# Rows of maxima one visit sooner, and a new order of the first instructions, in a decay-attention and expert kernel on one core

## The chip, the cores and the metric

The kernel runs on one core of one Trainium2 chip. The metric is the time of one execution on the device, in microseconds; the times shown are medians of several executions. Five engines work beside each other, each through its own row of instructions in a fixed order: TensorE (PE, matmuls; PEld are its weight loads), VectorE (DVE), ScalarE (ACT), GpSimd (POOL) and SyncE (SP), which here issues all DMAs. An instruction waits for what it needs of other engines, and all that stands behind it in its engine's row waits with it.

## The reference

Inputs are q, k, v of shape (8, 8, 576, 64) and f of shape (8, 8, 576), float32, and two weights, w_in (512 x 2048) and w_out (2048 x 512), which come as float64. Cut to what matters:

```
scores = matmul(q, k^T) / sqrt(64)
cum    = cumsum(log(clip(f, 1e-4, 1)))
scores = where(causal, -1e9, scores + cum[:, None] - cum[None, :])
scores = scores - max(scores)
attn   = exp(scores) / (sum(exp(scores)) + 1e-9)
y      = matmul(attn, v)                    # 8 x 8 heads
x      = y laid out as 4608 tokens x 512
h      = x @ w_in
g      = h * clip(h + 3, 0, 6) / 6
out    = g @ w_out
```

## The kernel before, in words

The kernel works through 68 **visits** (the list `VH`). Visits 0 to 3, "A", take two heads of batch 0 each and only their first 256 rows; visits 4 to 11, "B", take the other 320 rows of heads 0 to 7; visits 12 to 67, "F", take one whole head each of batches 1 to 7. Batch 0 is cut in two so that its first 256 tokens are ready early for the expert part, the MoE.

One visit consists of these steps:

- `load_x` (L409, L414): q and k of the visit come by DMA into ST. `load_c` (L420 to L430): the rows of the decay sums come into TK; for visits 0 and 1 they come straight from the tile `cs`, which DVE makes at L174 and L175, four DMAs in all.
- `parts` (L449, L450): POOL copies k into TK and q into TQ, rounded to the matmul's format. `rests` (L456 to L461): the rounded values are sent by DMA into T7 and T1, and POOL subtracts them from the unrounded ones, which leaves the low parts.
- For visits 0 to 11, `natural`: PE multiplies TQ by TK (L487, tile pn, one position of a row to a partition), and DVE takes the masked maximum of each 128 rows (L493, in pieces "junk") into MC. `max_rows`: PE transposes MC (L502, tile ptm), DVE negates it (L504, tile mr), and SP sends it as one row into partition 96 of TQ (L505).
- `scores`: PE multiplies again, the other way round, now with the row of maxima among the operands (L551), adds the products of the low parts (L552) and the mask (L554), into ps; ACT takes the exponential. For F visits `rows` does the work in another way: PE makes pn (L611, L614), DVE the masked maxima (L622, L628), ACT the exponential (L634, L648), DVE or POOL the split in high and low halves (L651, L657, L662).
- `av`: PE multiplies by v (L694 to L705, tile pav); DVE scales and splits the result (L726 to L738). `x_move` (L751, L755): DMA transposes bring it to the layout in which the expert part reads it.

The weights come in 32 chunks through a few tiles named ring, w and gT: a DMA (L238), an ACT step on the float64's upper half (L251), a shift (L252) and an or (L253) on DVE that make it float32, its squares for the scale (L257). Once the scale of all w_in is known (the reductions at L279, the transposition L184, the matrix eye at L317), PE makes w_in's low halves (L287, L288), DVE those of w_out (L295). v is loaded by L355 to L357, its largest value found at L366, and it is split at L400.

The expert part goes in units: h (PE L777 to L779, then ACT and DVE L783 to L788) and the output (PE L824 to L826, tile po). `done` appends the units of a half batch to a list, and `fill` takes some of them at many places of a visit, by a credit that each place adds to. `moe_out` of batch 0 first runs through what is left of the weights' work (`wq`).

What stands where in an engine's row is not the order of this text alone: the framework's scheduler takes the instructions in the order in which they are written as priorities and simulates when each can run, and each engine's row is what comes out. `tc.issue_after(x)` keeps what is issued in it behind x. One new order in the text can thus move instructions far behind it.

The loop over the visits, in the old kernel: at visit i it issues `load_x(i+3)`, `load_c(i+2)`, the first scores of visit i, `rests(i+1)`, `parts(i+2)`, then `max_rows(i+1)` in the middle, `natural(i+2)` in two halves, and last `av` of visit i-1. The `x_move` and `done` of a visit come in the middle of the visit after its `av` (`pend_x`).

Of the kernel before, what the change touches and what calls it, by code (L numbers as in the profile page):

```python
# [11 lines left out]
F32 = mybir.dt.float32  # L12
# [3 lines left out]
ALU = mybir.AluOpType  # L16
# [4 lines left out]
def kernel(  # L21
# [137 lines left out]
    def decay():  # L159
# [15 lines left out]
        nc.vector.scalar_tensor_tensor(  # L175
            cs[:, 1, :], cum, -8.0, cs[:, 0, :].bitcast(F32), op0=ALU.mult, op1=ALU.subtract
        )
        yield
# [63 lines left out]
    def w_decode(i, k, slots):  # L242

        slot = slots[k % len(slots)]
        f32 = w_chunk(i, k)[1]
        if wide:
            i32 = f32.bitcast(I32)
            hf = slot.bitcast(F32).rearrange("p (n t) -> p n t", t=2)[:, :, 1]
            lo = slot.rearrange("p (n t) -> p n t", t=2)[:, :, 0]

            nc.scalar.activation(f32, hf, AF.Prelu, scale=2.0 ** -112, alpha=2.0 ** 32)  # L251
            nc.vector.tensor_scalar(i32, i32, 3, None, op0=ALU.logical_shift_left)  # L252
            nc.vector.scalar_tensor_tensor(  # L253
                i32, lo, 29, i32, op0=ALU.logical_shift_right, op1=ALU.bitwise_or
            )
        if i == 1 or not GRAM[k // NCC]:
            nc.scalar.activation(  # L257
                slot.bitcast(F32)[:, :CW], f32, AF.Square,
                accum_out=wsum[:, NW * i + k:NW * i + k + 1],
            )  # L260
# [183 lines left out]
    def parts(v):  # L444
# [5 lines left out]
        nc.gpsimd.tensor_scalar(TQ[i][0:D, 0:nq], s[0:D, q0:q0 + nq], **one)  # L450
# [47 lines left out]
    def max_rows(v):  # L498
# [3 lines left out]
        nc.tensor.matmul(pt[:m, :P], MC[v % 2][:, 0:m], identr, start=True, stop=True)  # L502
# [3 lines left out]
        small.append(d.ins)  # L506

# [385 lines left out]
    next(dec)  # L893
    load_c(0)
    parts(0)
# [4 lines left out]
    init_qk(1, nc.gpsimd if INIT_POOL[1] else nc.vector)  # L900
    load_c(1)
    parts(1)
    for i in range(NL):
        nc.gpsimd.memset(T1[i].bitcast(F32)[:, S:], 0.0)
    max_rows(0)
    rests(0)
# [3 lines left out]
    natural(1, 0)  # L910
    if W_ORDER == 2:
        next(w_in_q)
    init_qk(2, nc.gpsimd if INIT_POOL[2] else nc.vector)
    nc.gpsimd.memset(v_chunk(0, 4)[64:], 0.0)
# [44 lines left out]
    for i, (kind, n) in enumerate(VH):  # L959
# [27 lines left out]
        if i + 1 < NV and VH[i + 1][0] != "F":  # L987
            max_rows(i + 1)
# [24 lines left out]
        fill(1)  # L1013
        if prev is not None:
            av(*prev)
            if VH[prev[0]][0] == "A" or VH[prev[0]][1] % 2 == 1:
                pend_x = prev[0]
        if n == H:
            v_split(n // 2)
# [45 lines left out]
```

## Time and profile before

| what | value |
| --- | --- |
| median of 3 executions | 1073.61 us (1069.77 to 1073.86) |
| the profiled execution's own time | 1069.33 us |
| its span, first to last instruction | 1067.5 us |
| granted TensorE clock, mean | 0.988 |
| PE busy | 1006.3 us (94%), 7650 matmuls |
| DVE busy | 731.1 us (68%) |
| ACT busy | 587.3 us (55%) |
| POOL busy | 403.4 us (38%) |
| DMA | 133.78 MB, mean 125 GB/s |

The windows view gives, for stretches of the span, the busy time of each engine with the count of instructions, the granted TensorE clock (1.00 is full), the mean busy share of the 16 DMA engines, and what they moved. The waits view gives an engine's idle time by what ended it: in all, how often, the longest. A timeline row is: start, duration, engine, line, operation, tiles; in brackets the idle time before it and what ended that. A row of the groups view has the busy time and the mean in ns of one after the first bar, the idle time before it after the second. Tiles' numbers are left out in all of them.

### The profile page before, as it was taken

How to read it: one execution, taken by the hardware profiler on the slowest of the kernel's cores; microseconds unless marked ns; L12 is line 12 of the kernel's file. 1: busy time of each engine (PE TensorE's matmuls, PEld its weight loads, DVE VectorE, ACT ScalarE, POOL GpSimd, SP SyncE). 2: the span in 40 equal slices, each digit the busy share in tenths (PEclk: the TensorE clock that was granted, in tenths of full speed). 3: DMA queues.
4: the chain of work that ended last, by engine and by line, in shares of the span. 5: the costliest groups of instructions: out<-in, count | busy, mean ns of one | idle time of the engine just before them, and what ended most of it. 6: DMA issues, size and time to landing. Idle time of an engine off the chain costs nothing.

```text
span 1067.5 us, 21157 instructions
## 1 busy us (share of the span) xinstructions
PE 1006.3 (94%) x7650; PEld 598.0 (56%) x7650; DVE 731.1 (68%) x1887; ACT 587.3 (55%) x1189; POOL 403.4 (38%) x505
## 2 busy tenths in 40 slices
PE   2799977899999999999999999999999999999897
PEld 1577844665555755555555755555555755444543
DVE  6978899996876768866886668846895677105300
ACT  4778666764764557545654557635764566115301
POOL 8343466443443444344443444534443330000000
PEclk9989989999999999999999999999999999999999
DMA  8965647955856776667575766566557554010000
GB/s 240 308 187 194 151 109 145 220 114 118 169 116 134 139 153 124 113 148 165 118 134 118 158 140 119 118 136 167 119 112 145 103 100 74 12 40 1 1 20 30
DMA packets 259155, 133.78 MB, mean 125 GB/s; under 512 B 226948, under 2 KB 228540, under 8 KB 259052
## 3 DMA queue, kind: packets, MB, share of 16 engines
q1 hardware_dynamic: 259052, 132.44, 55.7%
q8 instruction: 60, 0.98, 0.4%
q14 instruction: 43, 0.35, 0.1%
HBM read 47.93 MB, written 9.73 MB: 54 GB/s over the span
## 4 chain that ended last, share of the span: by engine, by line
PE 76%; DVE 12%; ACT 5%; issue 4%; DMA 2%; POOL 1%; SPq 0%; DVEq 0%; ACTq 0%; POOLq 0%
PE po L824 9%; PE po L826 9%; PE po L825 9%; PE ph L777 9%; PE ph L778 9%; PE ph L779 9%; PE pn L611 3%; PE pn L614 3%; DVE pp L622 2%; DVE ring L651 2%; PE po_r L826 1%; PE pav L698 1%; ACT pp L634 1%; PE po_r L824 1%; PE po_r L825 1%
## 5 line engine op out<-in xcount | busy, mean ns | idle before, releaser
L634 ACT ACTIVATE pp<-pp,nb 128x192 f32<-128x192 f32 x280 | 138.6, 552 | 170.3 <-DVE nb L628 150.8
L777 PE MATMUL ph<-xT,w 128*128 128x512 f16 (+1 forms) x576 | 198.8, 357 | 2.5 <-DVE r L786 2.4
L825 PE MATMUL po<-w,gT 128*128 128x512 f16 x512 | 192.6, 382 | 8.0 <-DVE w L295 8.0
L779 PE MATMUL ph<-xT,w 128*128 128x512 f16 (+1 forms) x576 | 198.0, 356 | 0.0
L778 PE MATMUL ph<-xT,w 128*128 128x512 f16 (+1 forms) x576 | 197.8, 356 | 0.0
L651 DVE TENSOR_TENSOR ring<-pp,ring 128x128 f16<-128x128 f32 (+2 forms) x216 | 138.0, 650 | 85.6 <-ACT ring L648 84.7
L824 PE MATMUL po<-w,gT 128*128 128x512 f16 x512 | 190.4, 383 | 5.8 <-DVE r_r L813 2.7
L826 PE MATMUL po<-w,gT 128*128 128x512 f16 x512 | 192.4, 383 | 0.0
L622 DVE CUSTOM_DVE_ANT_0 pp<-pn,W 128x192 f32<-128x192 f32 x280 | 123.3, 482 | 29.3 <-PE pn L614 28.0
L461 POOL TENSOR_TENSOR T<-ST,T 64x576 fp32r<-64x576 f32 (+1 forms) x68 | 100.9, 1483 | 107.2 <-DMA T<-TK 85.8
L786 DVE SCALAR_TENSOR_TENSOR r<-r,ph 128x512 f32<-128x512 f32 (+1 forms) x144 | 89.1, 620 | 61.4 <-ACT r L783 60.6
L611 PE MATMUL pn<-TK,TQ 68*128 68x192 f32 x336 | 124.8, 385 | 3.8 <-issue 2.2
L788 DVE TENSOR_TENSOR gT<-r,gT 128x512 f16<-128x512 f32 (+1 forms) x144 | 111.6, 781 | 22.0 <-ACT gT L787 20.6
L614 PE MATMUL pn<-T,T 128*128 128x192 f32 x336 | 115.2, 368 | 0.2 <-POOL T L461 0.2
L783 ACT ACTIVATE r<-ph,bias_r,SC 128x512 f32<-128x512 f32 (+1 forms) x144 | 103.9, 725 | 19.2 <-PE ph L779 17.1
L648 ACT CAST ring<-pp 128x192 f16<-128x192 f32 x280 | 114.2, 449 | 0.0
L787 ACT CAST gT<-r 128x512 f16<-128x512 f32 (+1 forms) x144 | 81.4, 567 | 59.6 <-DVE r L786 59.3
L449 POOL TENSOR_SCALAR TK<-ST 64x576 fp32r<-64x576 f32 (+1 forms) x68 | 49.2, 724 | 167.8 <-PE pn L611 142.9
L657 POOL TENSOR_TENSOR ring<-pp,ring 128x128 f16<-128x128 f32 x96 | 61.0, 636 | 116.1 <-ACT ring L648 75.2
L458 POOL TENSOR_TENSOR T<-ST,TQ 64x576 fp32r<-64x576 f32 (+2 forms) x68 | 95.2, 1400 | 17.7 <-PE pn L614 11.1
L826 PEld LDWEIGHTS <-gT 128*128 128x128 f16 x560 | 54.8, 98 | 74.5 <-issue 15.1
L825 PEld LDWEIGHTS <-gT 128*128 128x128 f16 x560 | 54.9, 98 | 66.5 <-issue 11.9
(158 smaller groups left out, 2010.2 us busy)
## 6 DMA issues: line engine op xcount, KB each, us to landing
ST<-in_qk_dram SPq DMA_DIRECT2D x64, 288.0 KB
T<-TK SPq DMA_DIRECT2D x64, 144.0 KB
ring<-in_w_out_dram SPq DMA_DIRECT2D x16, 512.0 KB
out_dram<-o SPq DMA_DIRECT2D x32, 256.0 KB
T<-TQ SPq DMA_DIRECT2D x56, 144.0 KB
vst<-in_vS_dram SPq DMA_DIRECT2D x7, 1040.0 KB
ring<-in_w_in_dram SPq DMA_DIRECT2D x9, 512.0 KB
w<-in_w_in_dram SPq DMA_DIRECT2D x7, 512.0 KB
```

Source lines behind the costliest of these rows:

```text
L611: nc.tensor.matmul(dst, TQ[i][0:D + 4, qs], TK[i][0:D + 4, a:e], start=True, stop=False)
L614: nc.tensor.matmul(dst, T7[j][:, qs], T1[j][:, a:e], start=False, stop=True)
L622: nc.vector.tensor_tensor_reduce(pp[:r, w:w + kw], pn[:r, o:o + kw], W[:r, 4 * P + r - kw:4 * P + r], 1.0, -3.0e38, ALU.add, ALU.max, accu ...
L634: nc.scalar.activation(x_, x_, AF.Exp, bias=nb[:r, e0 + x:e0 + x + 1], scale=0.125)
L648: nc.scalar.copy(hl[:r, h0[c]:h0[c] + kw], pp[:r, at[c]:at[c] + kw])
L651: eng.tensor_tensor(hl[:r, a:a + c * P], pp[:r, at[c] + 64:at[c] + kw], hl[:r, h0[c] + 64:h0[c] + kw], op=ALU.subtract,)
L777: nc.tensor.matmul(ph, w1[0][:, cc, fs_], xh, start=(cc == 0), stop=False)
L778: nc.tensor.matmul(ph, w1[0][:, cc, fs_], xl, start=False, stop=False)
L779: nc.tensor.matmul(ph, w1[1][:, cc, fs_], xh, start=False, stop=(cc == NCC - 1))
L824: nc.tensor.matmul(po, g[:, 0, fc, ts_], w2[:, fc, 0, :], start=(fc == 0), stop=False)
L825: nc.tensor.matmul(po, g[:, 0, fc, ts_], w2[:, fc, 1, :], start=False, stop=False)
L826: nc.tensor.matmul(po, g[:, 1, fc, ts_], w2[:, fc, 0, :], start=False, stop=(fc == NFC - 1))
```

## The change

Four things are changed. First, the shifts of the first three w_in chunks are kept behind the second row of `cs`. Second, the start has another order: POOL makes `parts(0)` before it clears the tiles of visits 1 and 2 or makes `rests(0)`, `max_rows(0)` is issued right after `natural(0, 0)`, `natural(1, 0)` is kept behind its transposition, and `max_rows(1)` is issued before the loop. Third, the loop issues `max_rows(i+2)` at the end of visit i, where it issued `max_rows(i+1)` in the middle: the rows of maxima of batch 0 are made and sent one visit sooner. Fourth, the last A pair's `x_move` and `done` come right after its `av`, not one visit later. The work itself is the same.

```diff
-        nc.vector.scalar_tensor_tensor(
+        last = nc.vector.scalar_tensor_tensor(
             cs[:, 1, :], cum, -8.0, cs[:, 0, :].bitcast(F32), op0=ALU.mult, op1=ALU.subtract
         )
+        small.append(last.ins)
...
-            nc.vector.tensor_scalar(i32, i32, 3, None, op0=ALU.logical_shift_left)
+            with tc.issue_after(after_cs) if i == 0 and k < 3 else nullcontext():
+                nc.vector.tensor_scalar(i32, i32, 3, None, op0=ALU.logical_shift_left)
...
     next(dec)
+    after_cs = small.pop()
     load_c(0)
-    parts(0)
+    p0 = parts(0)
...
     natural(0, 0)
-    init_qk(1, nc.gpsimd if INIT_POOL[1] else nc.vector)
+    m0 = max_rows(0)
+    with tc.issue_after(p0):
+        rests(0)
+        init_qk(1, nc.gpsimd)
+        for i in range(NL):
+            nc.gpsimd.memset(T1[i].bitcast(F32)[:, S:], 0.0)
     load_c(1)
-    parts(1)
-    for i in range(NL):
-        nc.gpsimd.memset(T1[i].bitcast(F32)[:, S:], 0.0)
-    max_rows(0)
-    rests(0)
+    p1 = parts(1)
     load_x(2)
     load_v(0)
     nc.sync.dma_start(scr, cs.bitcast(F32))
-    natural(1, 0)
-    if W_ORDER == 2:
-        next(w_in_q)
-    init_qk(2, nc.gpsimd if INIT_POOL[2] else nc.vector)
-    nc.gpsimd.memset(v_chunk(0, 4)[64:], 0.0)
+    with tc.issue_after(m0):
+        natural(1, 0)
+    max_rows(1)
+    with tc.issue_after(p1):
+        init_qk(2, nc.gpsimd)
+        nc.gpsimd.memset(v_chunk(0, 4)[64:], 0.0)
...
         ph = next(sg)
-        if i + 1 < NV and VH[i + 1][0] != "F":
-            max_rows(i + 1)
...
+        last_a = prev is not None and VH[prev[0]] == ("A", NPAIR - 1)
         if prev is not None:
             av(*prev)
             if VH[prev[0]][0] == "A" or VH[prev[0]][1] % 2 == 1:
                 pend_x = prev[0]
+        if last_a:
+            x_move(pend_x)
+            done(pend_x)
+            pend_x = None
+        if front:
+            max_rows(i + 2)
```

How the rows move on the engines, at three places. A number behind a tile's name tells copies of a tile apart; after the change the code's lines stand two or three lower.

SP at the start, before, from the cs rows of visit 0 to v's loads: the row of maxima of visit 0 (TQ0 from mr_0) stands ahead of the three loads from in_vS_dram.

```order
L430 DMA TK0_96<-cs_121 2x1x256 x2
L430 DMA TK1_97<-cs_121 2x1x256 x2
L456 DMA T70_101<-TQ0_93 64x512
L457 DMA T10_99<-TK0_96 64x512
L909 DMA decay_dram<-cs_121 64x1152
L238 DMA ring2_125<-in_w_in_dram 128x1024
L238 DMA w2_115<-in_w_in_dram 128x1024
L457 DMA T11_100<-TK1_97 64x512
L424 DMA TK2_98<-decay_dram 2x2x256
L456 DMA T71_102<-TQ1_94 64x512
L505 DMA TQ0_93<-mr_0_186 1x4x128
L355 DMA v16_111<-in_vS_dram 128x3x520
```

The same place on SP after:

```order
L432 DMA TK0_96<-cs_121 2x1x256 x2
L432 DMA TK1_97<-cs_121 2x1x256 x2
L357 DMA v16_111<-in_vS_dram 128x3x520
L358 DMA xT1_118<-in_vS_dram 128x520
L359 DMA xT1_118<-in_vS_dram 64x520
L914 DMA decay_dram<-cs_121 64x1152
L458 DMA T71_102<-TQ1_94 64x512
L459 DMA T11_100<-TK1_97 64x512
L239 DMA ring2_125<-in_w_in_dram 128x1024
L239 DMA w2_115<-in_w_in_dram 128x1024
L426 DMA TK2_98<-decay_dram 2x2x256
L411 DMA ST0_103<-in_qk_dram 128x2x256
```

The loads of v and the reload of ST0 stand ahead of the row of maxima now, which is the next row behind these.

DVE before, about the first row of maxima (the ISA rows are the masked maxima of L493, which leave their result in MC0 for visit 0 and MC1 for visit 1):

```order
L493 ISA MC1_107 128x1
L504 TENSOR_SCALAR mr_0_186<-ptm_0_184 4x128
L493 ISA junk_1_1_205,MC1_107<-pn_1_0_198,W_88 128x256
L493 ISA MC1_107 128x1
L252 TENSOR_SCALAR gT_116<-gT_116 128x512
L493 ISA junk_1_2_207,MC1_107<-pn_1_0_198,W_88 128x128
L493 ISA MC1_107 128x1
L253 SCALAR_TENSOR_TENSOR gT_116<-ring2_125,gT_116 128x512
L493 ISA junk_1_3_209,MC1_107<-pn_1_0_198,W_88 128x256
```

DVE after, from the third to the last maximum of visit 0 and to its row:

```order
L495 ISA junk_0_2_169,MC0_106<-pn_0_0_160,W_88 128x128
L495 ISA MC0_106 128x1
L368 TENSOR_REDUCE vm0_246<-v16_111 128x1
L281 TENSOR_REDUCE wm0_283<-wsum_122 128x1
L495 ISA junk_0_3_171,MC0_106<-pn_0_0_160,W_88 128x256
L495 ISA MC0_106 128x1
L368 TENSOR_REDUCE vm0_246<-xT1_118 128x1
L188 TENSOR_SCALAR e_w00_287<-pt_w00_285 128x1
L506 TENSOR_SCALAR mr_0_175<-ptm_0_173 4x128
```

Both reductions of v (L368) stand ahead of the row mr_0 now; before, they came behind the maxima of visit 1.

PE before, where the first output matmuls (po_0_0) of the first MoE half begin: behind the natural scores of visit 13.

```order
L611 MATMUL pn_13_1_1759<-TK1_97,TQ1_94 128x448
L614 MATMUL pn_13_1_1759<-T11_100,T71_102 128x448
L824 LDWEIGHTS gT_116
L824 MATMUL po_0_0_1376<-w2_115,gT_116 128x512
L824 LDWEIGHTS gT_116
L824 MATMUL po_0_1_1511<-w2_115,gT_116 128x512
L825 LDWEIGHTS gT_116
```

PE after, where po_0_0 begins: behind the second half of the scores of visit 10.

```order
L554 MATMUL ps_10_1_1519<-TQ1_94,TK1_97 128x64
L555 MATMUL ps_10_1_1519<-T70_101,T10_99 128x64
L557 LDWEIGHTS W_88
L557 MATMUL ps_10_1_1519<-ident16_80,W_88 128x64
L827 LDWEIGHTS gT_116
L827 MATMUL po_0_0_1331<-w2_115,gT_116 128x512
L827 LDWEIGHTS gT_116
```

The output matmuls of the first 256 tokens begin some three visits sooner in PE's row.

More of the change, by code (lines that the diff above doesn't have):

```diff
@@ L449, in parts @@
         nc.gpsimd.tensor_scalar(TK[i][0:D, 0:nk], s[D:, 0:nk], **one)
-        nc.gpsimd.tensor_scalar(TQ[i][0:D, 0:nq], s[0:D, q0:q0 + nq], **one)
+        return nc.gpsimd.tensor_scalar(TQ[i][0:D, 0:nq], s[0:D, q0:q0 + nq], **one).ins
     def rests(v):
@@ L501, in max_rows @@
         pt = ps_t.tile([P, 512], F32, tag="tr", name=f"ptm_{v}")
-        nc.tensor.matmul(pt[:m, :P], MC[v % 2][:, 0:m], identr, start=True, stop=True)
+        first = nc.tensor.matmul(pt[:m, :P], MC[v % 2][:, 0:m], identr, start=True, stop=True)
         mr = p2.tile([NCH, P], F32R, tag="mr", name=f"mr_{v}", bufs=1)
@@ L506, in max_rows @@
         small.append(d.ins)
+        return first.ins
     def pieces(v):
```

## The prediction

> **What bounds the kernel now.** I read the windows first, to find where TensorE (PE) is idle at all.
>
> ```profile
> core 0: us, PE busy (x) PEld busy (x) DVE busy (x) ACT busy (x) POOL busy (x), PEclk, DMA share, GB/s
> 0.00:60.00 60.00, 32.47 (x133) 24.22 (x134) 47.82 (x142) 37.40 (x77) 34.28 (x50) 0.93 0.85 260
> 10.00:20.00 10.00, 2.55 (x9) 1.86 (x9) 6.13 (x20) 3.90 (x10) 9.14 (x14) 1.00 0.75 205
> 20.00:40.00 20.00, 15.13 (x56) 11.75 (x57) 16.28 (x48) 11.80 (x24) 8.74 (x9) 1.00 1.01 331
> 50.00:60.00 10.00, 7.57 (x30) 5.29 (x29) 8.40 (x30) 8.52 (x18) 3.60 (x4) 0.56 0.72 213
> 60.00:140.00 80.00, 77.33 (x592) 64.16 (x590) 67.21 (x189) 55.87 (x117) 36.74 (x39) 0.99 0.62 175
> 140.00:210.00 70.00, 53.41 (x474) 33.63 (x472) 67.35 (x178) 49.03 (x108) 39.77 (x37) 0.90 0.75 159
> 140.00:150.00 10.00, 4.12 (x15) 1.62 (x13) 9.94 (x24) 6.29 (x15) 6.97 (x6) 0.67 0.26 72
> 200.00:250.00 50.00, 47.22 (x412) 32.61 (x410) 39.04 (x111) 29.87 (x70) 15.87 (x19) 1.00 0.68 140
> 400.00:1000.00 600.00, 597.46 (x4550) 333.30 (x4549) 400.95 (x999) 324.91 (x641) 210.52 (x277) 1.00 0.53 110
> ```
>
> From 400 to 1000 us PE is busy 597.46 of 600: there it is the bound, and a microsecond is won only by idling less elsewhere. It idles 27.5 us in the first 60 (60 less 32.47), 2.7 in the next 80, 16.6 from 140 to 210, where DVE is busy 67.35 of 70 and is the bound, and 2.8 from 200 to 250 (partly the same time). This pool of some 48 us is all that a new order of the front can draw on. The instruction orders of the two kernels are the same ones again from about the scores of visit 25, so that all of the effect is made before some 300 us and then carried unchanged to the end.
>
> What PE waited for in the first 260 us (us in total, times, longest) says who ends those gaps:
>
> ```profile
> PE pn L487 <- POOL TQ L450: 16.1, 2, 12.6
> PE po L825 <- DVE w L295: 8.0, 4, 3.8
> PE ps L551 <- DMA TQ<-mr: 4.3, 1, 4.3
> PE ptm L502 <- DVE MC L493: 2.2, 2, 1.3
> PE ps L551 <- DMA T<-TQ: 1.1, 1, 1.1
> ```
>
> The first natural scores wait 12.6 us for the q rows, the second ones 3.5 more; the first scores 4.3 us for the row of maxima that comes through DMA; and in the 140 to 210 stretch the output matmuls of the first MoE half wait 8.0 us for w_out's low halves, which DVE makes between the steps of the visits. The beginning in the order of time:
>
> ```profile
> 8.03 0.92 DVE L252 TENSOR_SCALAR gT<-gT 128x512 int32<-128x512 int32 x1 [0.62 <-ACT gT L251]
> 8.87 0.73 DVE L175 SCALAR_TENSOR_TENSOR cs<-cum,cs 64x576 fp32r<-64x576 f32 x1
> 9.69 2.67 SPq L430 DMA_DIRECT2D TK<-cs  x4
> 11.90 0.69 POOL L450 TENSOR_SCALAR TQ<-ST 64x512 fp32r<-64x512 f32 x1
> 12.64 1.22 PE L487 MATMUL pn<-TK,TQ 66*128 66x128 f32 x4 [12.64 <-POOL TQ L450]
> 14.52 0.54 SPq L238 DMA_DIRECT2D ring<-in_w_in_dram  x1
> 19.11 0.68 SPq L505 DMA_DIRECT2D TQ<-mr  x1
> 19.84 0.44 SPq L355 DMA_DIRECT2D v<-in_vS_dram  x1
> 20.40 0.66 ACT L251 ACTIVATE gT<-ring 128x512 f32<-128x512 f32 x1 [5.30 <-DMA ring<-in_w_in_dram]
> 22.94 0.58 PE L551 MATMUL ps<-TQ,TK 97*128 97x256 f32 x1 [4.29 <-DMA TQ<-mr]
> 25.69 1.75 DVE L366 TENSOR_REDUCE vm<-v 128x1 f32<-128x1536 f32 x1 [0.58 <-DMA v<-in_vS_dram]
> 27.62 1.20 DVE L366 TENSOR_REDUCE vm<-xT 128x1 f32<-128x1024 f32 x1
> 32.07 2.07 PE L287 MATMUL low<-gT,eye 128*128 128x512 f32 x2 [0.97 <-DVE eye L317]
> ```
>
> **The change part by part.** *The first natural scores (cs row ahead of three shifts, copies of visit 0 first on POOL).* DVE's second cs row loses the 0.92 us shift before it and the gap around it: it ends near 8.2 instead of 9.60, so SP can send the rows 1.4 us sooner; the q copy, late at 12.59, comes some 5 us sooner, since POOL no longer clears the other visits' tiles first. Now the rows from cs are late, where the copy was. Before, they had landed by 12.64, at most 2.95 us after their issue at 9.69. Issued near 8.3 they would land at 11.2 by that; but they share the queue with two q/k loads of 0.26 MB each, at most 0.52 MB at the 205 GB/s of 10 to 20 us, or 2.5 us, ahead of them. So the start of the natural scores lies between 11.2 and 13.8; I take 12.9, which is no gain, being nearest to the row in which they last had landed.
>
> *The row of maxima of visit 0.* It goes out after natural(0), with natural(1) behind its transposition; SP however now issues the three v loads ahead of it. v took 5.85 us from issue (19.84) to the reduction (25.69); issued near 11.5 it lands by 17.4. The two reductions of v, 1.75 and 1.20 us, now stand on DVE ahead of the first row of maxima, and the longer one ahead of visit 0's last maximum. 17.4 + 1.75 + 1.20 and about 0.8 for that maximum and the row make 21.1, and the row took 3.83 us from issue (19.11) to the scores (22.94): the first scores start near 25.0, that is 2 us later. It can be 23.5 where v comes over an emptier queue. Behind this wait PE isn't idle as before: the two pieces of the first w_in low half (2.07 us for two such matmuls) and the second visit's transposition are put ahead of the first scores, about 2.7 us of work. Net: 0.7 us won. From there the rows of maxima of visits 1 to 3 are a visit ahead: the waits for MC (2.2 us, of which the order can take 1.3) and for T (1.1) go, 2.4 us less. Against it stands the next thing late, the w_in pieces and PE's own work, which eats about half: 1.2. Start: 0.7 + 1.2, about **2 us won**. Bounds: 4 won (0.7 + 2.2 + 1.1), 3 lost (2 us later, 1 more of cover lost).
>
> *The queue's own order.* SP's waits are in program order. The row waits on DVE while behind it on SP stand the next two q/k loads and w_in chunks; before, the row stood ahead of v. Four w_in chunks are issued ahead of the later rows, some 5 us sooner, which is free: the DMA engines are full from 20 to 40 us (share 1.01) either way, so the order in which they are filled decides and not the sum.
>
> A row first, then a rule on it: between 10 and 20 us the queue's share was 0.75 and the maxima row of 2 KB still took 3.83 us. The Trainium skill, "DMA: Bandwidth & Descriptors", section "Queues, rings and completion order", says that on each DMA engine descriptors of a ring are consumed in ring order; by it a small row behind 1.2 MB of v pays for all that is still in the ring, up to 3.6 us at 331 GB/s, and the sum would be 3 us worse than mine if v were late by that much. This case's row shows a long small transfer, but not what lay ahead of it.
>
> *The last pair's rows at once; the first MoE half sooner.* The last A pair's transposes and the credits for the MoE's first half come a visit earlier, and with rows of maxima ahead the planner puts the first output matmul after the scores of visit 10 instead of after the natural scores of visit 13. PE's time from 60 to 140 us is full (77.33 of 80), so nothing is won there; what moves is what DVE has beside the w_out decoding from 140 on. The costs of DVE's steps between 130 and 205 us (mean ns after the comma):
>
> ```profile
> L622 DVE CUSTOM_DVE_ANT_0 pp<-pn,W 128x192 f32<-128x192 f32 (+4 forms) x35 | 15.4, 478 | 0.2
> L295 DVE SCALAR_TENSOR_TENSOR w<-w,SC 128x512 f16<-128x512 f32 x16 | 13.2, 824 | 0.4 <-ACT w L284 0.3
> L651 DVE TENSOR_TENSOR ring<-pp,ring 128x128 f16<-128x128 f32 (+2 forms) x20 | 12.5, 638 | 1.0 <-ACT ring L648 0.8
> L657 DVE TENSOR_TENSOR ring<-pp,ring 128x128 f16<-128x128 f32 x13 | 9.6, 735 | 0.0
> L400 DVE SCALAR_TENSOR_TENSOR v<-vst,SC,v 128x320 f16<-128x320 f32 x8 | 6.3, 803 | 0.0
> L628 DVE TENSOR_SCALAR nb<-MF 128x3 f32<-128x3 f32 (+1 forms) x14 | 3.8, 274 | 0.0
> L738 DVE TENSOR_TENSOR xhl<-xf,xhl 128x640 f16<-128x640 f32 (+1 forms) x3 | 3.4, 1122 | 0.0
> L622 DVE DVE_READ_ACCUMULATOR2_ANT MF<- 128x1 f32 (+1 forms) x35 | 2.7, 76 | 0.0
> L662 DVE TENSOR_TENSOR ring<-pp,ring 64x64 f16<-64x64 f32 x7 | 2.7, 381 | 0.0
> L366 DVE TENSOR_REDUCE vm<-vst 128x1 f32<-128x1024 f32 x1 | 1.2, 1203 | 0.0
> ```
>
> Between the first and the last of the sixteen w_out splits (L295) the old order has 25 masked maxima, 17 L651, 11 L657, 6 L662, 10 L628 and 3 L738; the new one 18, 9, 5, 3, 7 and 2. That is 7 x (0.478 + 0.076) = 3.9, 8 x 0.638 = 5.1, 6 x 0.735 = 4.4, 3 x 0.381 = 1.1, 3 x 0.274 = 0.8 and 1.1 less: 16.4. Five more v splits (L400: 4.0) and two more v reductions (2.4) come in, and about a dozen small scale steps of v, 1 us as an estimate from the rows of 0.08 to 0.27: 7.4 more. DVE has 9 us less to do while w_out is being made. That is the upper bound of this term, if DVE stays the bound to the end of it. The lower is zero, since the work isn't gone, only put behind: DVE has 11 us of slack from 200 to 250 (50 less 39.04) in which to do it. Of the 8.0 us of waits for L295 I take half, **4 us won**: the steps that stay ahead still alternate with the splits.
>
> *Coupling.* The nine microseconds put behind stand in front of the visits at 200 to 250, where PE idled 2.8 us. If they only fill the slack, they cost nothing; if PE waits for the visits' probabilities for part of it, up to 4. I take **2 lost**. Sum: -2 - 4 + 2 = **-4 us**, between -13 (4 and 9 won, nothing lost) and +7 (3 and 4 lost, nothing won).
>
> The profiled execution took 1069.33 us, with 1067.5 us of span; from it 1065.3. The three runs shown have a median of 1073.61, 4.3 above it, and the forecast against that is 1073.61 - 4 = **1069.6**.
>
> The clock is a term that I leave at nothing: 0.67 was granted from 140 to 150, with PE busy 4.12 of 10, 0.56 from 50 to 60, and 0.90 over 140 to 210. The Trainium skill, "TensorE: Matmul & The Clock Gate", part 1, puts the half clock on an idle window of about 3.4 us; by it a gap cut below 3.8 would also speed up the matmuls, by up to 0.10 x 53.41 = 5.3 us. That it helps needs PE to be the bound, which in this stretch it is not, so the sum stays.
>
> **The rivals.** *Full mixing (faster).* All of the 9 us goes and the slack takes what is postponed: -2 - 9 = -11, with the start's bounds -7 to -13: about 1063. For it speak the 8.0 us of waits on L295 and the 11 us of slack; against it, that the splits share DVE with whatever visit is under way.
>
> *DVE bounds the stretch whatever the order (no change).* Its work of 67.35 us in 70 is the same in sum; what is put behind from 140 to 210 comes due before 250, and the start's 2 us vanish into the same queue: 0, about 1073.6. For it: nothing is removed from DVE. Against it: the slack after 200.
>
> *The first scores wait longer, with every visit behind them (slower).* The place is the first row of scores on PE. Before them stands the transposition of visit 1's maxima, which waits for DVE, where a shift of the fifth w_in chunk (L252) stands ahead of the last maximum. That chunk was issued at 14.52 and decoded from 20.40; now 1.2 MB of v lies ahead of it in the queue, 3.6 us at 331 GB/s, so at most 24.0, and with T and cs rows ahead on SP later still. The mr row can be late in the same way. The price is the later start less its cover of 2.7: from 27 us on it decides. At 30 it is 30 - 22.94 - 2.7 = 4.4 lost at the start; the rest of the first visits is pushed by it and, with the coupling of 2 and no gain in the stretch, the time is +6, about 1080. For it speak the DMA share of 1.01 from 20 us; against, the 25% left free from 10 to 20.
>
> *That the rows aren't really sooner.* In the loop they are; in the prologue mr_0 is sent near 21.1 instead of 19.11: there the change does the contrary of its words. That is in the sum and the slower rival.
>
> **How the numbers follow.** Forecast 0.42 (-8 to 0: 1065.6 to 1073.6), full mixing 0.28, no change 0.13, slower 0.17. A measurement of this kernel can tell from no change about 0.5%, 5.4 us. Faster by more: nearly all of full mixing (0.27) and the low third of the forecast (0.13), 0.40. Slower by more: three quarters of the slower rival, 0.13. The rest, 0.47, is within. The range leaves out the most extreme fifth of full mixing (0.06) and most of the slower rival (0.13): 1061 to 1077.
>
> **What would show it.** Right: first natural scores at 12.5 to 13.3; first scores at 24 to 26 with PE busy over 4.5 us before them; waits on L295 at 4 us or less; PE idle before 300 us at about 44 instead of 48. Wrong: the first scores after 27, waits on L295 of 8 or more, or PE idling over 5 us from 200 to 250, which would show the postponed work as the new bound. If the first scores come before 23, the start was underrated.

## The result, and the profile after

The changed kernel takes 1077.67 us (median of 9 executions, 1075.84 to 1082.71), the old one beside it 1072.98 us (9, 1068.23 to 1073.91): a ratio of 1.0055, 95% interval 1.0039 to 1.0071. It is slower by about 0.5%, where 4 us less were forecast, and 0.7 us above the range. The profiled execution of the changed kernel took 1082.71 us and is the slowest of its nine, 5 us above their median; that of before, 1069.33 us, is 3.7 us below its own median. Of the 13.4 us between the two profiles some 9 are thus this choice, so the places of a loss are read from them, and their sizes only roughly. Of all executions below one, of after_pin0, took 3617.15 us, and its kernel's ratio leaves it out.

The windows, cut at three points that every variant passes: the first scores of visit 4, the first natural scores of visit 13, and those of visit 25, from where on the orders are the same. Before:

```profile
0.00:61.73 61.73, 34.20 (x138) 24.86 (x139) 47.82 (x142) 37.85 (x78) 34.76 (x51) 0.92 0.85 262
61.73:138.79 77.06, 74.39 (x576) 62.34 (x575) 66.00 (x187) 54.21 (x114) 35.12 (x39) 1.00 0.61 171
138.79:299.02 160.23, 141.88 (x1182) 87.77 (x1179) 140.17 (x367) 106.38 (x228) 79.65 (x86) 0.96 0.69 147
```

The same three stretches after, and some pieces of them:

```profile
0.00:67.95 67.95, 36.22 (x158) 25.83 (x158) 53.54 (x159) 44.04 (x92) 35.63 (x51) 0.83 0.83 262
67.95:154.43 86.48, 84.12 (x586) 65.39 (x587) 66.12 (x175) 51.86 (x105) 36.37 (x39) 0.94 0.50 138
154.43:310.83 156.40, 136.98 (x1147) 87.92 (x1147) 132.65 (x365) 103.70 (x225) 73.83 (x85) 0.95 0.73 149
34.00:40.00 6.00, 4.84 (x16) 3.39 (x16) 4.92 (x8) 5.69 (x13) 2.06 (x2) 0.56 1.03 340
40.00:46.00 6.00, 1.66 (x8) 1.18 (x6) 5.83 (x28) 4.77 (x12) 0.62 (x2) 0.50 1.04 338
46.00:50.00 4.00, 4.00 (x20) 3.71 (x20) 3.62 (x8) 4.00 (x9) 2.98 (x4) 0.50 0.97 371
60.00:68.00 8.00, 3.68 (x24) 2.50 (x22) 5.78 (x25) 6.13 (x13) 1.41 (x1) 0.84 0.84 241
68.00:80.00 12.00, 12.00 (x51) 8.06 (x51) 7.30 (x22) 7.29 (x16) 3.48 (x4) 0.68 0.49 132
240.00:300.00 60.00, 53.57 (x390) 29.65 (x389) 47.88 (x134) 38.34 (x79) 27.35 (x37) 0.94 0.83 163
```

The first number after the comma is PE's busy time; the stretch less it is PE's idle time: 27.5, 2.7 and 18.3 us before, 31.7, 2.4 and 19.4 after. The point at visit 25 comes at 310.83 us, not 299.02: 11.8 us later, of which 5.0 are idle time and 6.8 the longer run of PE's own work. PE does nearly the same matmuls up to there (1891, before 1896), and what differs with its busy time is the granted clock: 0.56 and 0.50 from 34 to 50 us, about a stretch in which PE had little to do (1.66 of 6 us), and 0.68 from 68 to 80, with PE busy all the time, right behind another such stretch (3.68 of 8). Before, the clock was down in this part from 50 to 60 us (0.56). The page's line on PE after:

```profile
PE 1014.9 (94%) x7650; PEld 602.5 (56%) x7650; DVE 727.7 (67%) x1887; ACT 587.7 (54%) x1189; POOL 398.4 (37%) x505
```

Before, the same 7650 matmuls were busy 1006.3 us. What PE waited for up to 300 us, after:

```profile
PE pn L489 <- DMA TK<-cs: 13.8, 1, 13.8
PE pt_w L185 <- DVE wm L281: 6.6, 2, 5.0
PE pn L614 <- issue: 6.5, 3, 4.2
PE ptm L504 <- DVE MC L495: 4.1, 4, 1.5
PE ps L554 <- DMA TQ<-mr: 2.8, 2, 1.4
PE po L828 <- DVE w L297: 2.3, 1, 2.3
```

The wait for w_out's low halves fell from 8.0 to 2.3 us, as forecast and by more. New are the waits for the scales of w_in (pt_w, 6.6 us), and the maxima's waits grew from 2.2 to 4.1. The start on SP, DVE and PE, after:

```profile
6.84 0.50 SPq L459 DMA_DIRECT2D T<-TK  x1
7.62 0.46 SPq L458 DMA_DIRECT2D T<-TQ  x1
8.22 5.25 SPq L432 DMA_DIRECT2D TK<-cs  x4
13.54 0.38 SPq L357 DMA_DIRECT2D v<-in_vS_dram  x1
17.86 0.67 SPq L239 DMA_DIRECT2D ring<-in_w_in_dram  x1
18.06 1.75 DVE L368 TENSOR_REDUCE vm<-v 128x1 f32<-128x1536 f32 x1 [1.55 <-DMA v<-in_vS_dram]
19.93 0.59 PE L185 MATMUL pt_w<-wm,ones 128*128 128x1 f32 x2 [4.96 <-DVE wm L281]
21.34 0.27 DVE L506 TENSOR_SCALAR mr<-ptm 4x128 fp32r<-4x128 f32 x1
21.63 0.69 SPq L507 DMA_DIRECT2D TQ<-mr  x1
26.46 0.52 PE L554 MATMUL ps<-TQ,TK 97*128 97x256 f32 x1
```

The four cs rows begin 1.5 us sooner than before (9.69), and end later: they took 5.25 us to issue instead of 2.67. The first row of maxima goes at 21.63 instead of 19.11, and the first scores start at 26.46 instead of 22.94. Ahead of the row stands v's reduction on DVE, and ahead of its transposition on PE the first scale, which waits 4.96 us behind that reduction. Some expectations below take these 5.0 us for a wait for the second scale, near 42 us; that one is 1.60 us long, and I had read the line of the waits without its place.

### The profile page after: what moved, and what is told of

Its sections match the earlier page's. It is cut to its first block, busy times and chain, and to the rows that moved or that the text cites. A ratio compares the mean times of both kernels' runs of the same rounds, so it can differ in the third digit from the quotient of the medians.

```text
span 1080.9 us, 21159 instructions
## 1 busy us (share of the span) xinstructions
PE 1014.9 (94%) x7650; PEld 602.5 (56%) x7650; DVE 727.7 (67%) x1887; ACT 587.7 (54%) x1189; POOL 398.4 (37%) x505
## 4 chain that ended last, share of the span: by engine, by line
PE 73%; DVE 11%; DMA 6%; ACT 4%; issue 4%; POOL 1%; SPq 0%; ACTq 0%; DVEq 0%; POOLq 0%
PE po L827 9%; PE po L829 9%; PE po L828 9%; PE ph L780 8%; PE ph L781 8%; PE ph L782 8%; PE pn L617 3%; PE pn L614 3%; DVE pp L625 2%; DVE ring L654 2%; DVE w L297 1%; PE po_r L829 1%; ACT pp L637 1%; PE po_r L827 1%; PE po_r L828 1%
## 5 line engine op out<-in xcount | busy, mean ns | idle before, releaser
L654 DVE TENSOR_TENSOR ring<-pp,ring 128x128 f16<-128x128 f32 (+2 forms) x216 | 141.1, 664 | 81.1 <-ACT ring L651 78.7
L791 DVE TENSOR_TENSOR gT<-r,gT 128x512 f16<-128x512 f32 (+1 forms) x144 | 108.1, 754 | 23.8 <-ACT gT L790 22.5
L660 POOL TENSOR_TENSOR ring<-pp,ring 128x128 f16<-128x128 f32 x96 | 58.2, 607 | 117.3 <-ACT ring L651 82.2
```

Source lines behind the costliest of these rows:

```text
L654: eng.tensor_tensor(hl[:r, a:a + c * P], pp[:r, at[c] + 64:at[c] + kw], hl[:r, h0[c] + 64:h0[c] + kw], op=ALU.subtract,)
```

## The experiments

In all of them the ratio is that to the old kernel, timed on the same chip in between. The last two columns are from their profiles. "Idle" is PE's idle time in the three stretches above, worked out from the windows in the same way; the expectations up to start_rests count it over those matmuls only that could be matched with the program, which at the scores of visit 4 gives some 6 to 8 us more (38.1 for start_only, 33.9 for before_v). The old kernel's median in these later sessions was 1070.28 to 1071.92 us; the row "before" is that of the result. Lines that only keep an instruction for later use are left out of the diffs.

| kernel | median us | ratio, interval | idle in the three stretches, us | PE busy in all, us |
| --- | --- | --- | --- | --- |
| before | 1072.98 | 1 | 27.5, 2.7, 18.3 | 1006.3 |
| after | 1077.67 | 1.0055, 1.0039 to 1.0071 | 31.7, 2.4, 19.4 | 1014.9 |
| loop_only | 1079.60 | 1.0066, 1.0042 to 1.0091 | 27.6, 7.6, 16.7 | 1014.0 |
| start_only | 1074.16 | 1.0021, 1.0003 to 1.0040 | 30.3, 2.9, 16.0 | 1010.8 |
| last_only | 1071.59 | 1.0000, 0.9982 to 1.0018 | 26.8, 1.5, 18.4 | 1012.3 |
| after_nolast | 1083.13 | 1.0119, 1.0090 to 1.0148 | 30.2, 2.4, 21.4 | 1011.3 |
| after_pin0 | 1070.35 | 0.9989, 0.9968 to 1.0010 | 27.5, 4.4, 13.2 | 1011.0 |
| before_pin0 | 1078.72 | 1.0073, 1.0046 to 1.0099 | 29.9, 5.6, 15.6 | 1013.7 |
| after_v | 1076.64 | 1.0048, 1.0028 to 1.0067 | 25.5, 4.5, 19.8 | 1011.4 |
| after_wact | 1078.45 | 1.0061, 1.0037 to 1.0085 | 31.5, 6.8, 17.1 | 1009.2 |
| after_mr2 | 1081.77 | 1.0096, 1.0063 to 1.0129 | 29.8, 3.4, 21.8 | 1014.2 |
| loop_wact | 1090.16 | 1.0177, 1.0146 to 1.0208 | 26.8, 6.6, 22.2 | 1021.8 |
| loop_chunk | 1080.38 | 1.0074, 1.0049 to 1.0098 | 26.9, 7.0, 18.3 | 1011.7 |
| before_rate62 | 1069.59 | 0.9991, 0.9970 to 1.0011 | 26.7, 2.9, 20.5 | 1004.4 |
| before_rate58 | 1071.10 | 1.0010, 0.9985 to 1.0035 | 27.0, 2.7, 18.3 | 1006.3 |
| before_v | 1064.89 | 0.9936, 0.9911 to 0.9961 | 27.7, 2.4, 13.9 | 1006.9 |
| start_v | 1078.16 | 1.0058, 1.0036 to 1.0081 | 28.2, 6.6, 16.5 | 1013.0 |
| before_v_last | 1070.86 | 0.9997, 0.9977 to 1.0018 | 28.9, 2.8, 15.7 | 1010.7 |
| start_rests | 1074.58 | 1.0029, 1.0009 to 1.0049 | 27.7, 3.8, 18.5 | 1009.9 |
| after_rests | 1070.71 | 0.9989, 0.9966 to 1.0012 | 26.8, 2.7, 17.6 | 1011.5 |

**The parts by themselves.** The first theories were that the loss is made by the new start (S), or behind 240 us by visits that were put off (P). loop_only is the old start with the third part of the change:

```diff
     natural(1, 0)
+    max_rows(1)
...
-        if i + 1 < NV and VH[i + 1][0] != "F":
-            max_rows(i + 1)
...
+        if front:
+            max_rows(i + 2)
```

Expected: 

> The old start; only the rows of maxima are issued a visit sooner (the row of visit 1 at the end of the prologue, then the row of visit i+2 at the end of visit i). Theory S (the loss is made in the first 85 us, by the new start: the loads of v ahead of the first row, the second group of w_in chunks late, a wait of 5.0 us for its scale, and the clock that falls with it): not slower than before, 1069 to 1074 against 1073. Theory P (the loss is made behind 240 us: the first MoE half is done sooner, the visits of batch 1 come later, and PE waits for their x, 4.2 us in the profile of after): slower, 1076 to 1078.

start_only is the change without its loop's part and without the last pair's:

```diff
-    max_rows(1)
...
+        if i + 1 < NV and VH[i + 1][0] != "F":
+            max_rows(i + 1)
...
-        if last_a:
-            x_move(pend_x)
-            done(pend_x)
-            pend_x = None
-        if front:
-            max_rows(i + 2)
```

Expected: 

> The new start, with the rows of maxima in the loop and the last pair's rows as before. Theory S: nearly all of the loss, 1076 to 1079 against 1073 before, with the scale of the second w_in group waited for by 4 to 6 us. Theory P: no loss, 1071 to 1074.

The loop alone loses as much as the whole, but not at the place of theory P: its three stretches are

```profile
0.00:62.85 62.85, 35.22 (x137) 26.17 (x138) 46.08 (x142) 37.31 (x77) 34.93 (x51) 0.89 0.87 254
62.85:148.63 85.78, 78.15 (x572) 64.06 (x570) 64.52 (x190) 54.07 (x116) 37.45 (x39) 0.96 0.57 160
148.63:310.33 161.70, 144.96 (x1184) 90.78 (x1183) 135.07 (x363) 105.90 (x227) 76.44 (x84) 0.95 0.67 143
```

The loss is in the middle one: 7.6 us idle where before had 2.7. Its waits from 70 to 140 us begin with the first h of the MoE, which waits for w_in's low half on ACT:

```profile
PE ph L777 <- ACT w L289: 4.0, 1, 4.0
```

start_only loses 0.2%, less than S said, and the two don't add up. The fourth part alone, and the change without it:

```diff
+        last_a = prev is not None and VH[prev[0]] == ("A", NPAIR - 1)
...
+        if last_a:
+            x_move(pend_x)
+            done(pend_x)
+            pend_x = None
```

Expected: 

> Before, with the last A pair's transposes and credits right after its av and nothing else. Theory P (the loss is made behind 240 us, since the first MoE half is sooner and the visits of batch 1 later): 2 to 5 us slower than before, with PE idle over 2 us between 240 and 300. Theory Q (the loss is made ahead of 140 us, where loads of weights stand on SP behind a load or a row that waits, and PE's row has the work that needs them too early): within 2 us of before, since nothing of SP's row ahead of 75 us moves.

after_nolast takes these five lines out of the changed kernel. Expected: 

> After, without that fourth part. Theory P: the idle time of 6 us behind 240 us goes, and the time falls by 4 to 6 us to 1072 to 1074. Theory Q: the idle time ahead of 140 us stays, and the time with it, 1076 to 1079.

last_only measures no difference, so that P falls; and without the fourth part the change gets slower, 1.0119. That part was not the cost of the change: with the other parts it was worth 6 us.

**Loads that are late.** after_pin0 and before_pin0 change what the loads of w_in chunks 4 to 7 are kept behind:

```diff
-        with pinned() if PIN or i == 0 and k < 8 else nullcontext():
+        with tc.issue_after(row_dma[0]) if i == 0 and 4 <= k < 8 else nullcontext():
```

Expected of after_pin0: 

> After, but the loads of w_in chunks 4 to 7 are kept behind the row of maxima of visit 0, not of visit 1. Theory S: they land some 4 us sooner, the wait for the second group's scale falls from 5.0 us to under 2, and the time falls by 3 to 6 us to 1072 to 1075. Theory P: as after, 1077 to 1078.

Expected of before_pin0: 

> Before, with the loads of w_in chunks 4 to 7 kept behind the row of maxima of visit 0 and not of visit 1: the control for after_pin0. If what after_pin0 won has to do with the new start, before wins nothing here, 1069 to 1073; if the sooner loads are worth it by themselves, it wins as much, some 7 us, to 1064 to 1066.

The first gave 7 us back, the second cost 0.7%. But what was to show the mechanism didn't: the wait for w_in's scale stayed in after_pin0, with

```profile
PE pt_w L185 <- DVE wm L282: 5.1, 1, 5.1
```

That line is the first scale again (its wait ends at 20.43 us), which the edit doesn't touch; the second's fell from 1.60 to 0.54 us, and the time by 7. The four loads did go sooner, from 22.87 us on instead of 27.68, but the wait named is not what was won. What was won shows when the stretch to visit 4 is cut at the first scores; before, after and after_pin0, two rows each:

```profile
0.00:22.94 22.94, 2.55 (x9) 1.86 (x9) 15.17 (x44) 9.96 (x19) 19.42 (x35) 1.00 0.78 230
22.94:61.73 38.79, 31.65 (x129) 22.99 (x130) 32.65 (x98) 27.89 (x60) 15.34 (x17) 0.87 0.89 281
0.00:26.46 26.46, 5.52 (x18) 3.63 (x18) 21.09 (x56) 11.69 (x22) 20.22 (x35) 1.00 0.79 252
26.46:67.95 41.49, 30.70 (x143) 22.20 (x141) 32.46 (x104) 32.35 (x71) 15.41 (x16) 0.72 0.86 267
0.00:26.31 26.31, 5.64 (x18) 3.69 (x18) 18.96 (x54) 10.68 (x21) 19.96 (x35) 1.00 0.80 260
26.31:64.22 37.91, 31.06 (x142) 22.05 (x141) 32.43 (x97) 30.73 (x67) 16.54 (x16) 0.84 0.81 261
```

Up to the first scores PE idles 20.4, 20.9 and 20.7 us, behind them 7.1, 10.8 and 6.9. So the start's loss lies behind the first scores, and the edit of the loads, with what the planner makes of it, takes it away, although all that is ahead stays as late in after_pin0 as in after: its four cs rows take 5.62 us to issue, its first natural scores start at 14.12 us and its first scores at 26.31.

Two more attempts at a late load or row, after_wact and loop_wact, let ACT issue the w_out chunks:

```diff
-                nc.sync.dma_start(slots[k % len(slots)], src.bitcast(I32))
+                (nc.scalar if i else nc.sync).dma_start(slots[k % len(slots)], src.bitcast(I32))
```

Expected of after_wact: 

> After, with the loads of the w_out chunks issued by ACT, whose square frees their tiles, and not by SP; they no longer stand behind rows and loads that wait there. Theory Q: the gaps from 70 us on get smaller, 3 to 6 us less than after, 1072 to 1074; those ahead of 70 us, where only w_in is loaded, stay. Theory P: as after, 1077 to 1078, or slower, since ACT issues sixteen DMAs more.

Expected of loop_wact: 

> The kernel with only the loop changed, with the loads of w_out issued by ACT. There a w_out chunk stood on SP behind the load of visit 7's q and k until 82.72 us (77.43 before), ACT's decode of it waited 4.74 us, and PE's first h waited 4.0 us behind that. If this chain is the loss of the loop's part: the 4.0 us go, and of the 7 us of loss at least 4: 1073 to 1075. If the wait only moves: 1077 to 1080.

Neither won. In loop_wact, the slowest of all, the wait of 4.0 us is gone and others have come; PE's busy time rose to 1021.8 us as well. after_mr2 keeps the shifts of w_in chunks 3 to 7 behind the row of maxima of visit 2 on DVE:

```diff
-            with tc.issue_after(after_cs) if i == 0 and k < 3 else nullcontext():
+            held = after_cs if i == 0 and k < 3 else row_op.get(2) if i == 0 and k < 8 else None
+            with tc.issue_after(held) if held else nullcontext():
```

Expected: 

> After, with DVE's shifts of w_in chunks 3 to 7 kept behind the row of maxima of visit 2, which stood behind four of them, and with it the scores of visit 2 planned ahead of the scale of the second w_in group. If the loss at the start is this queue on DVE (the row of visit 2 sent at 39.45 us in the profile of after, at 33.71 before): it is sent near 35, the 5.0 us wait for the scale goes below 2, and the time falls by 3 to 6 us to 1072 to 1075. If it is the order's chance: anywhere from 1070 to 1080, and the wait comes back elsewhere.

DVE made that row at 36.03 us then, but SP sent it late, behind two DMAs that waited, and the scores waited for it:

```profile
35.31 0.27 SPq L424 DMA_DIRECT2D TK<-decay_dram  x1
36.03 0.28 DVE L508 TENSOR_SCALAR mr<-ptm 4x128 fp32r<-4x128 f32 x1 [4.22 <-PE ptm L506]
36.51 0.47 SPq L460 DMA_DIRECT2D T<-TQ  x1
38.49 0.66 SPq L509 DMA_DIRECT2D TQ<-mr  x1
42.58 0.55 PE L556 MATMUL ps<-TQ,TK 97*128 97x256 f32 x1 [3.86 <-DMA TQ<-mr]
```

The second scale was waited for 0.53 us only, but the scores 3.86 us for the row, and the time rose. loop_chunk puts one neighbouring pair on SP back in the loop's variant:

```diff
-        if i + 3 < NV:
+        if i + 3 < NV and i != 7:
             load_x(i + 3)
...
             w_step()
+        if i == 7:
+            with tc.issue_after(w_dma[-1]):
+                load_x(i + 3)
```

Expected: 

> The kernel with only the loop changed, in which one neighbouring pair on SP is put back as before: the w_out chunk ahead of the load of q and k for visit 10 into ST1. If the wait of 4.0 us of the first h, with what hangs on it, is the loop's loss: the chunk is issued near 77.5 us and not at 82.7, the wait is under 1 us, and the time falls from 1079.6 to 1073 to 1075. If it is only one of several: 1076 to 1079.

The 4.0 us wait is gone, and the time didn't fall. The waits from 70 to 140 us are now led by

```profile
PE ph L778 <- DVE r L787: 4.2, 3, 2.7
```

The stretch still has 7.0 us of idle time. A single chain is not the loop's loss.

**The chance of an order.** If any new order of the work loses, a small meaningless change should too. before_rate62 and before_rate58 change the credits of one kind of visit:

```diff
-    F_RATE = (0.6, 0.45, 1.06)
+    F_RATE = (0.62, 0.45, 1.06)
```

Expected of before_rate62: 

> Before, with the first rate of credits 0.62 in place of 0.60: a change with no meaning of its own, which leaves the rows of all engines the same up to about 75 us and swaps a few neighbours behind that. Theory R (each new order of the same work lands on other waits of 2 to 5 us, since PE's row is planned with times that the chip doesn't keep, and the old order is a lucky one): off by 2 us or more, most likely slower, 1073 to 1077. Theory C (the loss is the contents of the change): 1069 to 1073, as before.

Expected of before_rate58: 

> Before, with that rate at 0.58, the same in the other direction. Theory R: off by 2 us or more again, 1073 to 1077. Theory C: 1069 to 1073.

Both are as before. Swaps of a few neighbours cost nothing; the orders that lose differ from the old one in much more.

**The new start.** By the count in the expectations, the profiles taken until then with v's loads ahead of the first row had 37 to 40 us of idle time up to visit 4, all others 31 to 35, and after_v the least. (In the table the split is not clean: after_pin0, with v ahead, has 27.5, and before_pin0, without, 29.9.) after_v keeps v's loads behind the row of visit 0:

```diff
-        with pinned() if PIN_V else nullcontext():
+        with (tc.issue_after(row_dma[0]) if b == 0 else pinned()):
```

Expected: 

> After, but v's three loads are kept behind the row of maxima of visit 0, as before the change. PE's row at the start becomes nearly that of before again, while the rows of visits 2 and later and the first MoE half stay sooner. Theory S: the loss at the start goes, 1068 to 1073. Theory P: as after, 1077 to 1078.

Its start idles 6.2 us less than after's, the rest 2.5 us more, and its time (1.0048) can't be told from after's. That seemed to put the start's loss down to v, which two runs tried from both sides. before_v:

```diff
+    load_v(0)
     max_rows(0)
     rests(0)
     load_x(2)
-    load_v(0)
```

Expected: 

> Before, with the three loads of v issued ahead of the row of maxima of visit 0 and nothing else: the new start's order of the loads in the old start. If v's place is what the new start loses by (at the first scores of visit 4 PE had idled 37.1 to 40.3 us in all five profiles that have v ahead of the row, and 31.5 to 35.4 in all that have not): PE has idled 37 us or more there, and the time is 2 to 6 us over before, 1073 to 1077. If the start loses by its other edits (the copies, the cs rows, natural(1, 0) behind the transposition): 1069 to 1073, as before.

start_v has the edit of after_v in start_only. Expected: 

> The new start without its order of v's loads (they are kept behind the row of visit 0), and neither the loop's nor the last pair's part. If v's place is the loss: PE has idled 31 to 33 us at the first scores of visit 4, and the time is 1067 to 1071, 0 to 4 below before, the 2 us that I had worked out for the start. If not: 1073 to 1076, as with the whole new start.

Both went the other way: v's loads ahead are worth 7 us in the old start, which makes before_v the fastest kernel of the study, and start_v lost 0.6%. So v's place is not the loss; whether another edit of the start is, was still to be tried. before_v reaches visit 13 at the same time as before (138.78 us) and wins in the stretch behind it, 154.75 us long instead of 160.23:

```profile
0.00:60.46 60.46, 32.77 (x158) 24.07 (x158) 51.37 (x154) 41.15 (x86) 34.54 (x50) 0.88 0.88 274
60.46:138.78 78.32, 75.88 (x553) 60.72 (x553) 62.03 (x174) 53.12 (x111) 34.98 (x38) 0.96 0.56 161
138.78:293.53 154.75, 140.84 (x1184) 90.24 (x1183) 133.73 (x369) 103.54 (x224) 79.19 (x86) 0.96 0.73 153
```

The next thing tried is the waits that the program gives to SP's rows. The DMAs use eight completion counters in turn (DMAHW0 to 7), and each waits until the one eight places ahead of it has landed. The changed kernel at the cs rows:

```
L459 DMA T10<-TK0   [waits DMAHW0, POOL]
L458 DMA T70<-TQ0   [waits DMAHW1, POOL]
L432 DMA TK0<-cs    [waits DMAHW2, DVE]
L432 DMA TK0<-cs    [waits DMAHW3]
L432 DMA TK1<-cs    [waits DMAHW4, POOL]
L432 DMA TK1<-cs    [waits DMAHW5]
```

Counters 2 to 5 belong to the first four w_in chunks, of 0.5 MB each. SP's own waits up to 30 us, after, show two of them at the cs rows:

```profile
SPq L432 <- DMA w<-in_w_in_dram: 2.1, 1, 2.1
SPq L432 <- DMA ring<-in_w_in_dram: 0.5, 1, 0.5
```

That is the 2.6 us by which the four rows took longer to issue. But these waits fell on the third and fourth row, of visit 1 (TK1), which went at 10.22 and 12.91 us. The first natural scores need visit 0's two rows (TK0) only, and these went at 8.22 and 9.03, hardly held at all. Before the change the cs rows stood two places further ahead, at counters 0 to 3, two of which were of f and the first q and k. start_rests and after_rests put the two DMAs of `rests(0)`, and with them POOL's two subtractions, back behind the cs rows:

```diff
     with tc.issue_after(p0):
-        rests(0)
         init_qk(1, nc.gpsimd)
...
     load_c(1)
+    with pinned():
+        rests(0)
     p1 = parts(1)
```

Expected of start_rests: 

> The start's part alone, with the two DMAs of rests(0) put back behind the four cs rows on SP. In the new start they stand ahead of them, and each DMA of SP waits until the one eight places ahead has landed, so that the four cs rows wait for the four w_in chunks: sent at 8.22, 9.03, 10.22 and 12.91 us in the profile of after. If that is what the new start loses by: the rows go at 8.2 to 10.5 us, the first natural scores start under 12.6 us, PE has idled under 35.5 us at the first scores of visit 4 (38.1 in start_only, 33.9 in before_v), and the time is 1064 to 1069. If it is another edit of the start: 1073 to 1076, as start_only.

Expected of after_rests: 

> The whole change with the same two DMAs put back behind the cs rows. If the start's queue is the whole loss of the change: 1064 to 1070. If the loop's part costs what it did with the old start, 7 us: 1072 to 1077.

The start in after_rests:

```profile
8.40 2.70 SPq L432 DMA_DIRECT2D TK<-cs  x4
11.14 0.53 SPq L458 DMA_DIRECT2D T<-TQ  x1
12.36 0.59 SPq L357 DMA_DIRECT2D v<-in_vS_dram  x1
16.07 0.28 DVE L506 TENSOR_SCALAR mr<-ptm 4x128 fp32r<-4x128 f32 x1 [0.36 <-PE ptm L504]
17.80 0.69 SPq L507 DMA_DIRECT2D TQ<-mr  x1
```

The cs rows issue in 2.70 us instead of 5.25, the first natural scores start at 12.2 us instead of 13.8, and the row of visit 0 goes at 17.80 instead of 21.63. Its stretches:

```profile
0.00:60.68 60.68, 33.84 (x158) 24.94 (x158) 52.46 (x149) 40.65 (x86) 38.01 (x51) 0.89 0.87 267
60.68:139.15 78.47, 75.74 (x538) 60.26 (x538) 62.46 (x169) 51.74 (x106) 33.82 (x36) 0.93 0.55 164
139.15:302.80 163.65, 146.07 (x1198) 92.64 (x1197) 139.94 (x380) 105.76 (x227) 81.61 (x89) 0.95 0.70 145
```

26.8 us idle to visit 4, where after had 31.7; the time is that of before (0.9989), 7 us under after. PE's idle time from 240 to 300 us is gone as well:

```profile
240.00:300.00 60.00, 60.00 (x448) 33.20 (x448) 47.84 (x126) 40.31 (x83) 30.50 (x38) 1.00 0.69 146
```

In the whole change, putting this pair back takes the loss away. What in it does so was not tried apart: the rows of visit 1 and v's loads behind them no longer wait for w_in chunks, the pair's 0.26 MB no longer lie ahead of visit 0's rows, and the new plan has the first row ahead of v's reduction on DVE, made at 16.07 us instead of 21.34. Nor is the pair's place enough for the loss: after_pin0 has it, with a start as late as after's, and loses nothing (0.9989 too). Two edits at different places take the same 7 us off, and whether by the same wait is open. In start_only the same edit has the same marks (12.27 us; 27.7 us idle instead of 30.3) and the time does not move: 1074.58 against 1074.16, where 1064 to 1069 would have shown the pair to be the start's loss; the 2.6 us are idled away later. And with the pair put back the loop's part and the last pair's together are not a cost: after_rests is 4 us faster than start_rests. before_v_last is before_v with the fourth part. Expected: 

> Before with v's loads ahead of the first row (before_v, 1064.9), and the last pair's part. If the parts add up, last_only having measured no difference: 1063 to 1067. If each part's worth hangs on the others: anything up to 1073.

It lost nearly all of the 7 us that before_v had won. None of these parts has a price of its own.

**What stays open.** Why the loop's part loses 7 us in the old start and nothing, with the last pair's part, on top of start_rests; which wait it is that after_pin0 and after_rests both take away; and why the same few microseconds won at the start reach the end in after_rests and not in start_rests: none of this is settled. The profiles show where the idle time is, and that each variant idles for other things; they don't show a rule by which one order keeps what it won.

## Why the prediction was wrong

Two terms of the sum failed in their direction: the start, 2 us won in the sum and 4.2 us of idle time lost in the profiles, nearly all of it behind the first scores; and the clock, left at nothing, with 6.8 us more of PE's busy time up to visit 25 in these two profiles. A third, the coupling, was too small. Why the new order idles more behind the first scores is known only in part.

- *The bound, and where the pool is.* Right in the main. From visit 25 on, all kernels but loop_wact take 767.5 to 771.1 us to the end (span less the point at visit 25); but for these 3.6 us, the differences are made ahead of it.
- *The first natural scores.* Mis-sized: 12.9 us taken, "no gain", and they came at 13.78, just inside the bounds. I had put the cs rows' lateness down to bytes ahead of them in the queue, and counted two q/k loads. The copies of `rests(0)` now stood ahead as well, and I had not priced them. With them put back, in after_rests, visit 0's rows go out no sooner (8.40 us, after 8.22) and the scores start at 12.23, 1.5 us sooner; 0.26 MB at the 205 GB/s that the prediction used are 1.3 us, an estimate. So bytes ahead are the likely reason here, and not the waits at issue, which held visit 1's rows.
- *The first row of maxima, from v.* Right in mechanism: made at 21.34 us behind v's reduction (from 18.06), 21.1 forecast; the scores started at 26.46, 25.0 forecast. PE idled some 0.5 us more up to there (20.9, before 20.4), where 0.7 were to be won. The row's 3.83 us, set beside a share of 0.75 from 10 to 20 us, began at 19.11 and fell nearly all in the stretch with the share 1.01. And a late row need not cost: before_v sends v first too, and is the fastest.
- *"From there the rows are a visit ahead", 2.4 us of waits less.* The step that failed. Behind the first scores PE idled 10.8 us up to visit 4 instead of 7.1, 3.7 more, where 1.2 were to be won. The waits for the maxima grew up to 300 us from 2.2 to 4.1, and the row of visit 2, a visit sooner in the program, went later in time, at 39.45 us instead of 33.71: DVE and SP had put work that waits ahead of it. Four w_in loads that are kept behind the row of visit 1 went from 27.68 us on; with them at 22.87, in after_pin0, the 3.7 us are gone. So in the whole change this loss hangs on where these loads stand. It is no rule: in the old kernel they went later still, from 28.64 us on, without such a loss, and sending them sooner there cost 0.7%.
- *The w_out stretch.* Right in direction and mechanism: the waits on L295 fell by 5.7 us, 4 were forecast. The idle time of the last stretch rose all the same, 18.3 to 19.4.
- *Coupling.* Mis-sized: 2 us were taken. From 200 to 250 us, the place named, PE idled 3.8 us instead of 2.8; but from 240 to 300 it idled 60 less 53.57, 6.4 us, where before it was busy throughout. In after_rests it is busy throughout again, and in after_pin0 it idles 0.7 us, with a start as late as after's: a late start alone doesn't make this loss.
- *The clock at nothing.* Wrong in these profiles. Stretches with little for PE to do came where PE is the bound right behind them, at 46 to 50 and 68 to 80 us, at a clock of 0.50 and 0.68, and PE's busy time rose by 8.6 us in all. How much of that is in the medians is open: after_v and after_pin0 have the same mean clock over their executions, 0.983 to 0.984, and lie 6 us apart. The Trainium skill, "TensorE: Matmul & The Clock Gate", part 1, puts the half clock on an idle window of about 3.4 us. The trace differs: PE's longest idle time between 26 and 80 us is 2.00 us, and the clock was down to 0.56 already from 34 to 40, with PE busy 4.84 of 6. Several shorter gaps went with the half clock here.
- *The signs.* Of the three that were to show the prediction wrong, none came (first scores at 26.46 us, waits on L295 of 2.3, 3.8 us idle from 200 to 250). None looked at the stretch from the first scores to visit 4, where most of the added idle time was.
- *The rivals.* The slower one named the time (1080) and the first scores as its place, with 27 us as its point; they came at 26.46, and before_v speaks against its mechanism (v ahead of the fifth w_in chunk and of the row). That its time was near is luck. None of the rivals had the w_in loads that are kept behind a later row.

## What to carry to other kernels

When code moves DMAs, count for each one the bytes that now lie ahead of it and the earlier DMA that it has to wait for at its issue: two copies put ahead of four small rows made SP wait 2.6 us here for loads of 0.5 MB. Before such a wait is called the loss, look for a run that has it and doesn't lose; after_pin0 is one. Take a part's price only together with the others: one edit (what four loads are kept behind) took 7 us off in one kernel and cost 8 in the other, so a part that measures nothing alone may be the one that saves the whole. And "one visit sooner" in the program is not sooner in time, if what is queued ahead of it has moved as well.

## What was not expected of the hardware

The same 7650 matmuls kept PE busy for 1004.4 to 1021.8 us in twenty profiles, 1.7%, with a mean granted clock of 0.974 to 0.989: for a kernel that PE bounds for 94% of its time, PE's own busy time is a term as large as the idle times that the changes move. It doesn't follow the mean clock alone: at 0.978 before_v_last has 1010.7 us and loop_wact 1021.8.
